# Storing the rows of a partial tile together, and dividing the last stores between two DMA queues

## The chip, the cores and the metric

The kernel runs on one core of a Trainium2 chip. The metric is the device time of one execution in microseconds (us). The engines that matter are TensorE (PE, matrix products), VectorE (DVE), ScalarE (ACT) and SyncE (SP). SP does no arithmetic: its queue issues DMA transfers. ScalarE's queue can issue them too, between its own instructions.

## The reference

A one-dimensional convolution with three taps over a sequence, batch normalisation with given statistics, and SiLU. B = 2, S = 2048, C = 1024, all bfloat16:

```python
xp = jnp.pad(x, ((0, 0), (1, 1), (0, 0)))
y = sum(jnp.einsum('bsc,cd->bsd', xp[:, k:k + S, :], w[k]) for k in range(3))
inv_std = 1.0 / jnp.sqrt(var + 1e-5)
y = (y - mean) * (g * inv_std) + b
return _silu(y)
```

## The kernel before

The convolution is computed by a minimal-filtering scheme: each group of R = 6 consecutive output rows needs eight products of transformed inputs and transformed weights instead of eighteen. A batch has NB = 342 such groups. As 2048 = 341 x 6 + 2, the last group holds only two rows; it is the partial tile of the change.

The inputs are loaded and transformed first. Then come 16 units of work, one for each block of 128 output channels (`dc`, eight) and batch (`bi`, two). `Unit.run` makes the eight products on TensorE, combines them on VectorE, and SiLU on ScalarE writes `yT`: 128 channels by 6 rows by 342 groups (padded to 384). The result has to be transposed before it is stored. The first 14 units do that with a DMA transpose (`turn`, line 439) and store with five DMAs (`store`, lines 451 and 455). The last two units are stored by `put` (line 409) instead: TensorE transposes 128 by 128 pieces into PSUM (line 419), VectorE or ScalarE copies them into a tile `o` (line 420), and each block of 128 groups is stored by one DMA (line 425).

The groups of a batch make three blocks: 0 and 1 of 128 groups and block 2 of 85 full groups and the partial one. `put` is called for `inner` rows 1 to 4 of each group and for `outer` rows 0 and 5, as these become ready at different times. Whenever a call covers the last block, it also stores the row of the partial group that its rows hold: row 1 in an inner call, row 0 in an outer call, one DMA of a single row of 256 bytes each (line 431).

The order of all instructions is written by hand; each engine runs its own in that order. The very last unit is cut in two halves, `h0` (groups 128 to 341, blocks 1 and 2) and `h1` (groups 0 to 127, block 0). The unit before it is `prev`. The kernel's last lines (526 to 539) call `put` for these three, and the last argument names the queue of each block's store, `sp` or `ac`.

Each DMA is given one of eight DMA semaphores by the framework. It is issued only once the previous DMA on the same semaphore has landed. In the built program the stores from line 533 on, with the number of the semaphore that each holds, are:

| queue | stores in order (semaphore) |
|---|---|
| SP | h0 inner block 1 (4), h0 inner block 2 (5), h0 row 1 (6), h0 outer block 1 (7), h0 outer block 2 (0), h0 row 0 (1), h1 outer (2) |
| ScalarE | h1 inner (2) |

A store of an inner block is 128 groups (85 in block 2) by 4 rows by 256 bytes, an outer one 2 rows. The four stores before these on SP are those of `prev`: outer block 2, row 0, inner block 2, row 1.

Of the kernel before, what the change touches and what calls it, by code (L numbers as in the profile page):

```python
# [15 lines left out]
P = 128  # L16
R = 6
# [9 lines left out]
def kernel(  # L27
# [11 lines left out]
    B, S, C = x.shape  # L39
# [29 lines left out]
    rows = consts.tile([4 * DC, P], BF16, name="rows")  # L69
# [217 lines left out]
    class Unit:  # L287
# [121 lines left out]
        def put(self, o, rows, bank, evac, queues, blocks=None):  # L409

            i0, i1 = min(rows), max(rows)
            every = slice(i0, i1 + 1, 1 if i1 == i0 else (i1 - i0) // (len(rows) - 1))
            blocks = blocks or range(self.lo // P, -(-self.hi // P))
            n = min(self.hi - self.lo, P)
            v = ps[:, bank].bitcast(BF16)[0:n, 0:len(rows) * len(blocks) * P]
            v = v.rearrange("p (i k d) -> p i k d", i=len(rows), k=len(blocks))
            for a, i in enumerate(rows):
                for q, k in enumerate(blocks):
                    nc.tensor.transpose(v[:, a, q], self.yT[:, i, k * P:k * P + n], ident)  # L419
            evac(o[0:n, every, blocks[0]:blocks[-1] + 1], v)  # L420
            outs = out[self.bi, :, self.dc * P:(self.dc + 1) * P]
            full = S // R
            for q, k in zip(queues, blocks):
                hi = min((k + 1) * P, full)
                q.dma_start(
                    out=outs[k * P * R:hi * R].rearrange("(p i) d -> p i d", i=R)[:, every],
                    in_=o[0:hi - k * P, every, k],
                )
                cut = [i for i in rows if i < S % R]
                if hi == full and cut:  # L430
                    q.dma_start(
                        out=outs[full * R + cut[0]:full * R + cut[-1] + 1].rearrange("(p i) d -> p i d", p=1),
                        in_=o[full - k * P:full - k * P + 1, cut[0]:cut[-1] + 1, k],
                    )

        def turn(self, pool=opool):

# [60 lines left out]
    for i, (dc, bi) in enumerate(seq[:-1]):  # L498
# [20 lines left out]
        before, prev = prev, unit  # L519
    dc, bi = seq[-1]  # L520
    sp, ac = nc.sync, nc.scalar
    inner, outer = tuple(range(1, R - 1)), (0, R - 1)
    to_v, to_s = nc.vector.tensor_copy, nc.scalar.copy
    o = olast.tile([P, R, NK, P], BF16, name="o")
    h0 = Unit(dc, bi, 4, P, NB)
    h0.run(between, prev.rest(between, 5, 5) + [(5, lambda: prev.put(o, inner, 1, to_v, (sp, sp), (0, 1)))])
    h1 = Unit(dc, bi, 0, 0, P)
    h1.run(between, [
        (2, lambda: prev.put(o, outer, 2, to_s, (sp, sp, sp))),
        (3, lambda: prev.put(o, inner, 1, to_s, (sp,), (2,))),  # L530
    ] + h0.rest(between, 5, 6))
    o2 = olast.tile([P, R, NK, P], BF16, name="o")
    h0.put(o2, inner, 5, to_v, (sp, sp))
    h1.silu_inner()
    h1.first(between)
    h1.last(between)
    h0.put(o2, outer, 6, to_v, (sp, sp))
    h1.put(o2, inner, 1, to_v, (ac,))
    h1.put(o2, outer, 2, to_v, (sp,))

_INS = ['x', 'w', 'mean', 'var', 'g', 'b']
_OUTS = [((2, 2048, 1024), 'bfloat16')]
# [24 lines left out]
```

## Time and profile before

| | |
|---|---|
| median of 3 runs | 193.5 us (193.17 to 193.84) |
| profiled execution | 193.33 us, span 191.6 us |
| mean granted TensorE clock | 0.991 |
| TensorE busy | 177.4 us, 93% of the span |
| VectorE, ScalarE busy | 156.8 us, 111.5 us |
| DMA moved | 31.71 MB |
| TensorE's last transpose ends | about 185.05 us |
| VectorE's last copy starts | 185.09 us |

The span runs from the first to the last instruction. Times in the timeline count from its start. A line of the timeline gives start, length, engine, line in the kernel and what is written from what; SPq and ACTq are the queues of SP and ScalarE, where the length of a DMA is that of its issue and not of its transfer. A line of the windows gives the stretch, its length, the busy time of PE, weight loads, DVE, ACT and POOL, the granted clock, the mean busy share of the 16 DMA engines and what they moved in GB/s. A line of the waits gives who waited for whom, the sum in us, the number of waits and the longest.

### The profile page before, as it was taken

To read this page: it belongs to the slowest core of one execution; us is meant where nothing else is said; L and a number is where in the kernel's file an instruction comes from. 1 tells how busy PE (TensorE), PEld (TensorE's weight loads), DVE (VectorE), ACT (ScalarE), POOL (GpSimd) and SP (SyncE) were. 2 spreads that over 40 slices of the span, in tenths; PEclk is the share of its full clock that TensorE was granted. 3 is DMA by queue.
4 is the path that set the end of the run, shared out by engine and by line. 5 is a ranking of instruction groups with operands and counts; after the bars stand their busy time and mean duration, and the time that the engine had idled before them with its cause. 6 is when DMAs were issued, how large, how long until landed. Compare 5 with 4: busy or idle time off the path is not lost.

```text
span 191.6 us, 3716 instructions
## 1 busy us (share of the span) xinstructions
PE 177.4 (93%) x1397; PEld 126.7 (66%) x1397; DVE 156.8 (82%) x222; ACT 111.5 (58%) x187; POOL 136.8 (71%) x76
## 2 busy tenths in 40 slices
PE   1998879999999999999999999999999999999960
PEld 1976758666666666666666666666666666678940
DVE  5589866789978799988998899879988996767960
ACT  3689977774546565465545554656274663636750
POOL 5579999806796879999999999699999780000000
PEclk9999999999999999999999999999999999999996
DMA  5999998084142838499759577969587396948652
GB/s 201 309 332 331 346 330 261 8 224 109 32 91 50 184 66 171 136 225 205 137 119 185 110 151 208 214 145 193 110 168 152 81 123 140 206 110 127 142 134 58
DMA packets 86800, 31.71 MB, mean 166 GB/s; under 512 B 73406, under 2 KB 82622, under 8 KB 86782
## 3 DMA queue, kind: packets, MB, share of 16 engines
q1 hardware_dynamic: 86190, 31.33, 71.8%
q8 instruction: 11, 0.18, 0.4%
q10 hardware_dynamic: 592, 0.14, 0.3%
q14 instruction: 7, 0.06, 0.1%
HBM read 14.82 MB, written 8.39 MB: 121 GB/s over the span
## 4 chain that ended last, share of the span: by engine, by line
PE 83%; DMA 7%; ACT 2%; SPq 2%; DVE 1%; issue 1%; ACTq 0%
PE ps L311 78%; DMA xw<-in_x_dram 6%; PE ps L265 5%; DMA rows<-in_g_dram 1%; SPq L130 1%; ACT T_sb L276 1%; PE ps L419 1%; DVE o L420 1%; ACT w1x L162 0%; DVE T_sb L278 0%; SPq L146 0%; ACTq L71 0%; ACT w1x L180 0%
## 5 line engine op out<-in xcount | busy, mean ns | idle before, releaser
L311 PE MATMUL ps<-T_sb,u 128*128 128x342 bf16 (+2 forms) x816 | 120.0, 299 | 0.3
L311 PEld LDWEIGHTS <-u 128*128 128x128 bf16 x816 | 76.8, 97 | 33.6 <-issue 0.6
L194 POOL TENSOR_TENSOR u<-e,w1x 128x1024 bf16<-128x1024 f32 x32 | 70.3, 2223 | 12.5 <-DVE e L176 12.4
L311 PE MATMUL ps<-T_sb,wch 128*128 128x342 bf16 (+2 forms) x272 | 42.5, 299 | 0.0
L334 ACT ACTIVATE yT<-ps,beta,scale 128x342 bf16<-128x342 f32 (+5 forms) x51 | 34.0, 704 | 11.8 <-PE ps L311 11.8
L329 DVE SCALAR_TENSOR_TENSOR t<-ps,sd 128x684 f32<-128x684 f32 (+2 forms) x51 | 39.1, 822 | 0.6
L194 POOL TENSOR_TENSOR u<-e,wch 128x1024 bf16<-128x1024 f32 x16 | 37.6, 2369 | 1.0 <-DMA wch<-in_w_dram 0.4
L311 PEld LDWEIGHTS <-wch 128*128 128x128 bf16 x272 | 25.7, 97 | 11.5
L322 ACT COPY pc<-ps 128x342 f32<-128x342 f32 (+2 forms) x34 | 14.5, 426 | 31.9 <-PE ps L311 31.2
L265 PE MATMUL ps<-rm,xw 128*128 128x168 bf16 (+1 forms) x256 | 26.1, 250 | 6.6 <-DVE rm L100 3.9
L276 ACT CAST T_sb<-ps 128x672 bf16<-128x672 f32 (+1 forms) x37 | 25.8, 735 | 7.4 <-PE ps L265 7.3
L278 DVE CAST T_sb<-ps 128x672 bf16<-128x672 f32 x29 | 23.5, 854 | 7.6 <-PE ps L265 7.6
L265 PEld LDWEIGHTS <-xw 128*128 128x128 bf16 (+1 forms) x256 | 21.4, 105 | 11.3 <-DMA xw<-in_x_dram 5.5
L329 DVE SCALAR_TENSOR_TENSOR ps<-ps,t 128x684 f32<-128x684 f32 (+2 forms) x34 | 28.3, 832 | 0.6
L176 DVE SCALAR_TENSOR_TENSOR e<-wch 128x1024 f32<-128x1024 bf16 x14 | 27.2, 1941 | 0.0
L329 DVE SCALAR_TENSOR_TENSOR ps<-ps,pc 128x342 f32<-128x342 f32 (+2 forms) x34 | 16.9, 498 | 8.9 <-PE ps L311 7.1
L174 POOL TENSOR_TENSOR e<-wch 128x1024 f32<-128x1024 bf16 x8 | 19.0, 2370 | 3.5 <-DMA wch<-in_w_dram 3.4
L334 ACT ACTIVATE yT<-t,beta,scale 128x684 bf16<-128x684 f32 (+2 forms) x17 | 15.7, 925 | 0.0
L329 DVE SCALAR_TENSOR_TENSOR sd<-pc,ps 128x342 f32<-128x342 f32 (+2 forms) x17 | 8.3, 487 | 8.4 <-ACT sd L322 8.3
L329 DVE SCALAR_TENSOR_TENSOR t<-ps,t 128x684 f32<-128x684 f32 (+2 forms) x17 | 13.9, 818 | 0.0
L322 ACT COPY sd<-ps 128x342 f32<-128x342 f32 (+2 forms) x17 | 7.3, 428 | 10.2 <-PE ps L311 10.2
L324 ACT ACTIVATE pc<-ps 128x342 f32<-128x342 f32 (+2 forms) x17 | 7.5, 440 | 9.4 <-PE ps L311 5.9
(39 smaller groups left out, 38.0 us busy)
## 6 DMA issues: line engine op xcount, KB each, us to landing
xw<-in_x_dram SPq DMA_DIRECT2D x30, 256.0 KB
out_dram<-o SPq DMA_DIRECT2D x28, 192.0 KB
wch<-in_w_dram SPq DMA_DIRECT2D x9, 512.0 KB
out_dram<-o SPq DMA_DIRECT2D x14, 120.0 KB
wch<-in_w_dram SPq DMA_DIRECT2D x6, 256.0 KB
xfirst<-in_x_dram SPq DMA_DIRECT2D x2, 224.0 KB
out_dram<-o SPq DMA_DIRECT2D x3, 128.0 KB
out_dram<-o SPq DMA_DIRECT2D x4, 64.0 KB
```

The lines of the kernel that those rows point to most:

```text
L130: nc.sync.dma_start(out=xw[0:hi - lo, :], in_=x[bi, lo:hi, :])
L174: eng.tensor_tensor(e, w0, w2, op=ALU.add)
L176: eng.scalar_tensor_tensor(out=e, in0=f, scalar=4.0, in1=h, op0=ALU.mult, op1=ALU.add)
L194: nc.gpsimd.tensor_tensor(u[:, i], sums[dc, q], o, op=op)
L265: nc.tensor.matmul(v[:, c * nb // nct, c % (nct // nb)], lhsT=xw[0:rows, (c0 + c) * P:(c0 + c + 1) * P], rhs=rm[0:rows, :, 0:n], start=Tru ...
L276: nc.scalar.copy(dst, src)
L278: nc.vector.tensor_copy(dst, src)
L311: nc.tensor.matmul(self.bank[q], lhsT=lhsT, rhs=T_sb[:, ct, j, nsl], start=not add and ct == 0, stop=ct == CT - 1, skip_group_check=add,)
L322: nc.scalar.copy(dst, self.bank[q])
L324: nc.scalar.mul(dst, self.bank[q], by)
L329: nc.vector.scalar_tensor_tensor(out=out, in0=in0, scalar=scalar, in1=in1, op0=ALU.mult, op1=op1)
L334: nc.scalar.activation(self.yT[:, rows, self.lo:self.hi], src, ACT.Silu, bias=beta[:, dc:dc + 1], scale=scale[:, dc:dc + 1])
```

## The change

`put` no longer stores rows of the partial group. A new method `put_cut` stores both of its rows by one DMA of two rows, once for `prev` and once for `h0`. Of the last unit's stores, h0's outer block 2 and h1's outer store are issued by ScalarE instead of SP.

```diff
@@ put
-                cut = [i for i in rows if i < S % R]
-                if hi == full and cut:
-                    q.dma_start(
-                        out=outs[full * R + cut[0]:full * R + cut[-1] + 1].rearrange("(p i) d -> p i d", p=1),
-                        in_=o[full - k * P:full - k * P + 1, cut[0]:cut[-1] + 1, k],
-                    )
+
+        def put_cut(self, o, queue):
+
+            full = S // R
+            k, p0 = full // P, full % P
+            queue.dma_start(
+                out=out[self.bi, full * R:S, self.dc * P:(self.dc + 1) * P].rearrange("(p i) d -> p i d", p=1),
+                in_=o[p0:p0 + 1, 0:S % R, k],
+            )
@@ the last unit
-        (3, lambda: prev.put(o, inner, 1, to_s, (sp,), (2,))),
+        (3, lambda: prev.put(o, inner, 1, to_s, (sp,), (2,))), (3, lambda: prev.put_cut(o, sp)),
...
     h0.put(o2, inner, 5, to_v, (sp, sp))
...
-    h0.put(o2, outer, 6, to_v, (sp, sp))
+    h0.put(o2, outer, 6, to_v, (sp, ac))
     h1.put(o2, inner, 1, to_v, (ac,))
-    h1.put(o2, outer, 2, to_v, (sp,))
+    h0.put_cut(o2, sp)
+    h1.put(o2, outer, 2, to_v, (ac,))
```

In the built program the stores of the last unit then stand as follows:

| queue | stores in order (semaphore) |
|---|---|
| SP | h0 inner block 1 (4), h0 inner block 2 (6), h0 outer block 1 (7), h0 two rows (0) |
| ScalarE | h0 outer block 2 (1), h1 inner (3), h1 outer (5) |

The stores of `prev` before these on SP are outer block 2, inner block 2 (semaphore 0) and its two rows (2). TensorE's, VectorE's and GpSimd's orders are as before.

## The prediction

> **What bounds the kernel now.** I read the page first, to see whether the change can touch the body. TensorE is busy for 177.4 us of the 191.6 us span, so the body is a TensorE chain. The changed lines only issue stores at the very end.
>
> ```profile
> span 191.6 us, 3716 instructions
> PE 177.4 (93%) x1397; PEld 126.7 (66%) x1397; DVE 156.8 (82%) x222; ACT 111.5 (58%) x187; POOL 136.8 (71%) x76
> ```
>
> So the tail is what counts. The chain of waits, in order of time, ends with VectorE's last copy into `o2`, at 185.09 + 0.29 = 185.4 us. The profile follows nothing past it, yet the span runs 6.2 us longer. In that time only stores are under way. The timeline of the tail, SP's queue and ScalarE's (start us, length us, queue, line):
>
> ```profile
> 183.18 0.25 SPq L431 DMA_DIRECT2D out_dram<-o  x1
> 183.54 0.28 SPq L425 DMA_DIRECT2D out_dram<-o  x1
> 183.87 0.42 SPq L431 DMA_DIRECT2D out_dram<-o  x1
> 184.39 0.39 SPq L425 DMA_DIRECT2D out_dram<-o  x1
> 184.84 0.39 SPq L425 DMA_DIRECT2D out_dram<-o  x1
> 185.09 0.42 ACTq L425 DMA_DIRECT2D out_dram<-o  x1
> 185.28 0.48 SPq L431 DMA_DIRECT2D out_dram<-o  x1
> 185.85 1.13 SPq L425 DMA_DIRECT2D out_dram<-o  x1
> 187.03 0.36 SPq L425 DMA_DIRECT2D out_dram<-o  x1
> 187.44 0.37 SPq L431 DMA_DIRECT2D out_dram<-o  x1
> 188.82 0.39 SPq L425 DMA_DIRECT2D out_dram<-o  x1
> ```
>
> The last line is the store of h1's outer rows. Its data have been ready since 185.4, but it is issued at 188.82, 3.4 us later. Two things hold it: SP's seven issues before it, which end at 187.81 (one of them takes 1.13), and then a wait. The waits of SP's queue from 187.5 on:
>
> ```profile
> SPq L425 <- DMA out_dram<-o: 0.9, 1, 0.9
> SPq L562 <- DMA out_dram<-o: 1.3, 1, 1.3
> ```
>
> The first is this store waiting for its DMA semaphore (number 2 of eight). ScalarE's store of 185.09, h1's inner rows, holds the same semaphore, and by the trace's record of semaphore increments its last one comes at 188.75. The second is the kernel's end waiting for the last store: from 189.26 to 190.49. Then 191.55 - 190.49 = 1.06 us of closing steps follow. The windows show the transfers (last two columns: share of the 16 DMA engines, GB/s):
>
> ```profile
> 184.50:185.00 0.50, 0.38 (x3) 0.17 (x2) 0.50 (x2) 0.27 (x1) 0.00 (x0) 1.00 0.33 71
> 185.50:186.00 0.50, 0.00 (x0) 0.00 (x0) 0.00 (x0) 0.00 (x0) 0.00 (x0) 1.00 0.87 198
> 188.50:189.00 0.50, 0.00 (x0) 0.00 (x0) 0.00 (x0) 0.00 (x0) 0.00 (x0) 0.50 0.12 26
> 189.00:189.50 0.50, 0.00 (x0) 0.00 (x0) 0.00 (x0) 0.00 (x0) 0.00 (x0) 0.50 0.02 5
> 189.50:190.00 0.50, 0.00 (x0) 0.00 (x0) 0.00 (x0) 0.00 (x0) 0.00 (x0) 0.50 0.48 112
> ```
>
> Traffic dies out by 189.5 and starts again for the late store alone. While only an 85-row store is moving (184.5 to 185.0), a third of the engines work, at 71 GB/s. A 128-row store uses all of them, at 198/0.87 = 228 GB/s. So 85-row stores load a narrow group of engines, and that group finishes last.
>
> **The change part by part.**
>
> *Four one-row stores go, two two-row stores come.* SP loses 0.25 + 0.42 + 0.48 + 0.37 = 1.52 us of issues. The nearest row for a two-row store is line 455, which has the same form: 14 issues of 640 to 647 ns. Two cost 1.28 us, so this part frees SP of 0.24 us. It is not on the path that sets the end.
>
> *h0's outer store of block 2 goes to ScalarE.* ScalarE's queue gets it before the store that it has now. VectorE's three last copies start at 184.25, 184.63 and 185.09, so its data are ready at 184.6. It can be issued at 184.65, for 0.36 us by its SP row. Its semaphore was last used by the 30-row store of 178.68, long landed. Behind it on ScalarE stand only two more stores, as all activations come earlier in that queue. The h1 inner store therefore still starts at about 185.09, when its copy ends.
>
> *h1's outer store goes to ScalarE.* It now follows the h1 inner store, at 185.09 + 0.42 + 0.05 = 185.56. The built program gives it semaphore 5, last used by a store of the unit before (issued 181.32, landed by 183.24). The 0.9 us wait is gone, and so is its place behind SP's issues. It is issued 3.26 us earlier, which would be the gain if nothing else were late. But the same bytes have to move.
>
> *What is late next: the narrow group.* Its time for each store, in full bytes (256 B a row piece): 85 x 4 pieces, 87 kB at 71 GB/s, 1.22 us; 85 x 2, 0.61; 128 x 4, 131 kB at 228 GB/s, 0.58; 128 x 2, 0.29.
> Test on the trace of before: the 85-row store issued at 183.54 starts to move at about 184.35 (18 GB/s in 184.0 to 184.5, then 71), 0.81 after its issue. Behind it the group has 1.22 + 0.58 + 1.22 + 0.58 + 0.29 + 0.61 = 4.50 us of work: it should end at 188.85. The row of 188.5 to 189.0 shows just that fall, to 26 GB/s.
> After the change, that store of the unit before takes the place of the one-row store at 183.18 (its copy has been done since 180.54), and moves from 183.18 + 0.81 = 184.0. The group has 0.29 more, the h1 outer store's share: 4.79 us, to 188.8. It doesn't starve: SP issues the two-row store at about 183.5 to 184.15, h0's inner stores at 184.2 and 184.65, h0's outer block 1 at 185.1, and ScalarE's are out by 186. Even an issue that is held up for 1.13 us meets a group with work waiting.
>
> *The trailing engine.* In before the stores of 187.03 and 187.44 land last at 189.47 and 189.65 by the increments, although the group's other engines have posted theirs by 189.01. One engine runs some 0.45 to 0.65 us behind. Its cause isn't settled: one-row stores that need this engine, or instruction loading (packets of 16 KB and 8 KB at 183.0 and 183.75 on the instruction queues, 0.88 and 0.42 us long). If the lag were all the one-row stores', the end would come at 189.0; if it stays, at 189.5 to 189.6. I take that it stays, as the 8 KB packet's 0.42 us is nearest to it: 189.65 - 0.05 (group end 188.8 instead of 188.85) = 189.6, less up to 0.2 as no one-row store stands last: 189.5.
>
> *h0's two-row store* waits for semaphore 0, which the unit before's 85-row store holds. That was issued at 183.54 in before and landed at 185.88, 2.34 us later; from 183.18 that gives 185.5, when SP's issue before it has just ended (185.5). It costs nothing then, and nothing but the kernel's end is behind it.
>
> *Sum.* The last landing moves from 190.47 to 189.5, by 1.0 us. The profiled execution took 193.33 (span 191.6 plus 1.7 around it): 192.3. The three runs have a median of 193.5, 0.17 above; I predict 192.4, between the two ends 192.3 and 192.5. Bounds of the gain: 1.5 (landing at 189.0), and 0.5 (the trailing engine another half us later, as much again as its lag now).
>
> **A rule weighed.** The row is the 3.4 us that finished data waited in SP's queue. The Trainium skill, page "DMA: Bandwidth & Descriptors", section "Issuing engines are not separate DMA queues", speaks against the change: stores started by several engines run on the same 16 DMA engines, and a second issuer saves only issuing time. By it the gain would be the issues moved off SP, 0.36 + 0.39 = 0.75 us, so 192.6. This trace agrees on shared engines, but not that only issuing is saved, for 0.9 us of the delay is a semaphore wait.
>
> **The rivals.**
>
> *More: the lag was the one-row stores'.* For it: they land up to 3.65 us after issue (185.28, at 188.93). Against: the instruction packets are as long as the lag. The end is at 189.0 or a little before, a gain of 1.5 to 1.8: 191.7 to 192.0. Chance 0.2.
>
> *Less: ScalarE's issues are held up.* For it: one SP issue took 1.13 us in this tail, and a store on line 451 1.44. Three in a row of 1.13 from 184.65 end at 188.1 with their gaps; the last store took 1.26 us from the end of its issue to landing (189.21 to 190.47) with idle engines; here it adds to the trailing engine, at up to 190.0. Gain 0.4 to 0.6: 192.9 to 193.1. Against: ScalarE's only store in this tail took 0.42. Chance 0.17.
>
> *Slower: the last two-row store ends the kernel.* It stands last on SP. If its issue, behind the full group, is held by 1.44 us twice (h0's outer block 1 and then itself, 185.1 to 188.0), and it then needs the 3.65 us that the one-row store of 185.28 needed from start to landing, 3.2 from the end of its issue, it lands at 191.2, 0.7 later than now: 194.0. It decides from a landing after 190.47. Against: that store's long time was the queue ahead of it, which by 188 is nearly empty. Chance 0.06.
>
> The change not doing what it says can be left out: the built order has both moves, and TensorE's and VectorE's orders are unchanged.
>
> **How the numbers follow.** The forecast, a gain of 0.6 to 1.5, has the remaining 0.57, its own range 192.0 to 192.9. Within 0.3% (0.58 us) is about what a measurement of this kernel can't tell from no change; the runs before alone spread by 0.35%. Faster: 0.57 + 0.2 and a third of the second rival, less a little for that spread: 0.81. Slower: 0.05. Same: 0.14. The range for 8 in 10 runs from 191.6 (the first rival, less 0.1 of run to run) to 193.1 (most of the second).
>
> **What would show it.** ScalarE's queue with three line-425 stores at about 184.65, 185.1 and 185.6; no SP wait of 0.9 on line 425; full-width traffic ending by 188, a thin tail to 189.2, and no second burst; the closing wait ending at about 189.5. It is wrong if ScalarE's issues stretch past 187, if the closing wait ends after 190, or if a fall in the span comes from before 183.

## The result and the profile after

The changed kernel takes 192.66 us (median of 13 runs, 192.02 to 193.34) against 193.5 us before (13 runs). The ratio is 0.9952, with a 95% interval of 0.9932 to 0.9973: 0.9 us faster, between 0.5 and 1.3. The profiled execution took 192.30 us with a span of 190.5 us.

TensorE and the other engines do the same work as before:

```profile
span 190.5 us, 3715 instructions
PE 177.3 (93%) x1397; PEld 126.5 (66%) x1397; DVE 157.6 (83%) x222; ACT 111.2 (58%) x187; POOL 136.8 (72%) x76
```

In this execution VectorE's last copy into `o2` ends at 185.17, 0.21 earlier than in the one of before. That is drift between executions: the code ahead of it is the same, and over all executions below this copy ends between 185.2 and 186.5. So two tails are compared from the end of that copy. From there to the last landing it is 190.47 - 185.38 = 5.09 us before and 189.56 - 185.17 = 4.39 us after. (Landings, here and below, are read from the trace's record of semaphore increments; a store adds up to 16 of them, one for each DMA engine that it runs on; a store on fewer engines has one entry more, ahead of these, which isn't counted here.)

The timeline of the tail, first SP's queue from the store of `prev`'s inner block 2 on, then ScalarE's (start us, length us, queue, line):

```profile
183.28 0.27 SPq L425 DMA_DIRECT2D out_dram<-o  x1
183.61 0.64 SPq L434 DMA_DIRECT2D out_dram<-o  x1
184.35 0.40 SPq L425 DMA_DIRECT2D out_dram<-o  x1
185.23 0.28 SPq L425 DMA_DIRECT2D out_dram<-o  x1
185.60 0.53 SPq L425 DMA_DIRECT2D out_dram<-o  x1
186.18 1.30 SPq L434 DMA_DIRECT2D out_dram<-o  x1
184.49 0.30 ACTq L425 DMA_DIRECT2D out_dram<-o  x1
184.89 0.52 ACTq L425 DMA_DIRECT2D out_dram<-o  x1
185.50 0.48 ACTq L425 DMA_DIRECT2D out_dram<-o  x1
```

The last issue starts at 186.18 where it started at 188.82. It is the two-row store of h0, and it is held for 1.30 us. h1's outer store, the last line, goes out at 185.50. The waits of SP's queue from 182.5 on:

```profile
SPq L566 <- DMA out_dram<-o: 2.0, 2, 1.5
SPq L425 <- DMA out_dram<-o: 0.5, 1, 0.5
```

The first is the closing wait: SP has issued everything by 187.5 and waits for landings until 189.59. The second is new. h0's inner block 2 waits for semaphore 6, whose holder was issued at 181.89; 15 of its increments are there by 183.64, the last comes at 185.21.

The windows (last two columns: busy share of the 16 DMA engines, GB/s):

```profile
186.50:187.00 0.50, 0.00 (x0) 0.00 (x0) 0.00 (x0) 0.00 (x0) 0.00 (x0) 1.00 0.99 225
187.50:188.00 0.50, 0.00 (x0) 0.00 (x0) 0.00 (x0) 0.00 (x0) 0.00 (x0) 0.50 0.52 112
188.00:188.50 0.50, 0.00 (x0) 0.00 (x0) 0.00 (x0) 0.00 (x0) 0.00 (x0) 0.50 0.37 83
188.50:189.00 0.50, 0.00 (x0) 0.00 (x0) 0.00 (x0) 0.00 (x0) 0.00 (x0) 0.50 0.32 71
189.00:189.50 0.50, 0.00 (x0) 0.00 (x0) 0.00 (x0) 0.00 (x0) 0.00 (x0) 0.50 0.02 3
189.50:190.00 0.50, 0.00 (x0) 0.00 (x0) 0.00 (x0) 0.00 (x0) 0.00 (x0) 0.50 0.00 0
```

The second burst of before, 112 GB/s in 189.5 to 190.0, is gone. In its place the last microsecond runs on a third of the engines, at 71 to 83 GB/s: the narrow group, working off its queue. The stores land at 188.94 (h0 inner block 2), 189.15 (h1 outer), 189.39 (h0 outer block 1) and 189.56 (the two rows).

So the time is won in the tail. Which of the two edits won it, and what limits the tail now, is what the experiments ask.

### The profile page after: what moved, and what is told of

It reads as the page before. It is cut to its first block, busy times and chain, and to the rows that moved or that the text cites. A ratio compares the mean times of both kernels' runs of the same rounds, so it can differ in the third digit from the quotient of the medians.

```text
span 190.5 us, 3715 instructions
## 1 busy us (share of the span) xinstructions
PE 177.3 (93%) x1397; PEld 126.5 (66%) x1397; DVE 157.6 (83%) x222; ACT 111.2 (58%) x187; POOL 136.8 (72%) x76
## 4 chain that ended last, share of the span: by engine, by line
PE 82%; DMA 5%; ACT 4%; DVE 3%; SPq 2%; issue 1%; DVEq 0%
PE ps L311 76%; PE ps L265 5%; DMA xw<-in_x_dram 5%; DVE T_sb L278 3%; ACT yT L334 2%; SPq L130 2%; ACT T_sb L276 1%; SPq L146 1%; PE ps L419 1%; ACT w1x L162 0%; ACT o L420 0%; DVE o L420 0%; ACT w1x L180 0%; ACT pc L322 0%; DVEq L278 0%
## 5 line engine op out<-in xcount | busy, mean ns | idle before, releaser
L176 DVE SCALAR_TENSOR_TENSOR e<-wch 128x1024 f32<-128x1024 bf16 x14 | 28.0, 2000 | 0.0
```

Of the source, the lines that this page charges most:

```text
L176: eng.scalar_tensor_tensor(out=e, in0=f, scalar=4.0, in1=h, op0=ALU.mult, op1=ALU.add)
```

## The experiments

Two theories on the gain. A: the late store was late because of a semaphore that it shared with h1's inner store, and a change that breaks the sharing wins the gain; what is left is the narrow group's work. B: the gain comes from dividing the stores between two queues, as SP's was too long.

### Only the merged store

From the changed kernel, the two queue edits are undone:

```diff
-    h0.put(o2, outer, 6, to_v, (sp, ac))
+    h0.put(o2, outer, 6, to_v, (sp, sp))
...
-    h1.put(o2, outer, 2, to_v, (ac,))
+    h1.put(o2, outer, 2, to_v, (sp,))
```

> Only the one-row stores are merged; all queues are as before, so h1's outer store stands last on SP. Theory A (the end is set by when the last store may be issued and by the narrow group's bytes, and the semaphore wait is what mattered): merging alone changes which semaphore the last store holds (0, whose holder before it lands by about 185.9), so the 0.9 us wait is gone without any change of queue. SP issues it after the two-row store, at 187.5 to 188.1 instead of 188.82, landing at 189.2 to 189.8: 0.6 to 1.2 us faster than before, ratio 0.994 to 0.997. Theory B (the division between the queues makes the gain): only SP's issue time is saved, 0.24 us, ratio 0.999.

Measured: ratio to before 0.9947 (0.9918 to 0.9976). All of the changed kernel's gain is here, with no store moved between queues. SP's last three issues:

```profile
186.37 0.92 SPq L425 DMA_DIRECT2D out_dram<-o  x1
187.34 0.60 SPq L434 DMA_DIRECT2D out_dram<-o  x1
188.04 0.39 SPq L425 DMA_DIRECT2D out_dram<-o  x1
```

The wait ahead of the last one is gone. h1's outer store follows the two-row store at once, 188.04 - 185.69 = 2.35 us after the last copy, against 3.44 before. Its semaphore had been free since 186.33. The issues ahead of it end 2.25 us after the last copy, against 2.43 before, so of the 1.09 us some 0.2 are issuing and the rest is the wait. Merging two rows of 256 bytes acts on the time mainly through the numbering of the semaphores. The landing gains less in this execution: 15 of the last store's increments are there by 189.69, within the 189.2 to 189.8 that A gave, but the sixteenth comes at 190.32, 4.6 us after the last copy.

This run also tells something of the trailing engine. There are no one-row stores in this tail, and one engine of the narrow group still trails: of h0's inner block 2 four increments are there by 188.54 and the last comes at 189.30.

### Every store on SP

From the kernel before, the other way round: ScalarE issues nothing in the tail.

```diff
-    h1.put(o2, inner, 1, to_v, (ac,))
+    h1.put(o2, inner, 1, to_v, (sp,))
```

> Before, with every store of the last unit on SP: nothing is issued by ScalarE at all, the one-row stores stay. The eight semaphores then go round on one queue, and h1's outer store no longer shares one with h1's inner store. Theory A (the semaphore wait made the loss, not the length of SP's queue): SP issues h1's inner store after the one-row store, at about 187.9, and h1's outer at 188.3 instead of 188.82; it lands at 189.9 to 190.2, 0.3 to 0.6 us faster than before although SP has more to do, ratio 0.997 to 0.9985. Theory B (the division between the queues makes the gain): one more store on SP, 0.4 us slower than before or worse, ratio 1.002 and up.

Measured: ratio 0.9941 (0.9911 to 0.997). It is faster than expected, and B's 1.002 is outside the interval. SP's last three issues:

```profile
187.22 0.38 SPq L431 DMA_DIRECT2D out_dram<-o  x1
187.69 0.39 SPq L425 DMA_DIRECT2D out_dram<-o  x1
188.19 0.45 SPq L425 DMA_DIRECT2D out_dram<-o  x1
```

SP issues one store more than before, and h1's outer store still goes out 188.19 - 185.58 = 2.6 us after the last copy instead of 3.4, as the eight semaphores now go round in the order of one queue and none is waited for. Not all of this is the semaphore: h0's outer block 1 took 0.39 us to issue here and 1.13 before. From the last copy to the last landing it is 4.39 us, as in the changed kernel. In the kernel before it was the one store on ScalarE that made the two share a semaphore.

### Only the queues, and only the last store

Both start from the kernel before and keep the one-row stores. The first divides the queues as the change does:

```diff
-    h0.put(o2, outer, 6, to_v, (sp, sp))
+    h0.put(o2, outer, 6, to_v, (sp, ac))
...
-    h1.put(o2, outer, 2, to_v, (sp,))
+    h1.put(o2, outer, 2, to_v, (ac,))
```

> Only the queues are divided; the one-row stores stay (row 0 of h0 goes to ScalarE with its block). Theory A: h1's outer store is out by 186.2, but the semaphores fall differently: h0's outer block 1 on SP now waits for semaphore 2, which ScalarE's h0 outer block 2 holds until it lands at about 187. It is issued at about 187.1 and lands at about 189.0, when the narrow group ends anyway: closing wait ends at 189.3 to 189.7, 0.8 to 1.2 us faster than before, ratio 0.994 to 0.996. Theory B says the same size, 0.994 to 0.996; a theory that the one-row stores are the delay (they trail by 0.45 to 0.65) says 0.998 to 1.000.

Measured: 0.9973 (0.9947 to 1.0), less than either theory gave, though the interval reaches into what all three gave, so this run doesn't part them. The waits of SP's queue from 183 on show a new wait:

```profile
SPq L562 <- DMA out_dram<-o: 2.1, 1, 2.1
SPq L425 <- DMA out_dram<-o: 1.6, 1, 1.6
```

It isn't the one that I had expected. h0's inner block 1 has fallen on semaphore 6, held by `prev`'s outer block 1. That store has 15 increments by 184.24 and the sixteenth at 186.45. So SP stands still from 184.89 to 186.52, with h0's stores behind. One late engine of an earlier store holds SP's queue for 1.6 us here, because the semaphore numbers fell so.

The second moves h1's outer store alone:

```diff
-    h1.put(o2, outer, 2, to_v, (sp,))
+    h1.put(o2, outer, 2, to_v, (ac,))
```

> Before, with h1's outer store alone moved to ScalarE. Theory A: the wait is handed on. h0's row 0, last on SP, now gets semaphore 2 and has to wait for ScalarE's h1 inner store until about 188.75, so a store of 256 bytes ends the kernel, landing at 190.0 to 190.5: 0 to 0.5 us faster than before, ratio 0.9975 to 1.000. Theory B (SP's queue was too long; taking one store off it helps): 0.8 to 1.0 us faster, ratio 0.995.

Measured: 0.9985 (0.9964 to 1.0005). The size is the one that A gave, and B's 0.995 lies outside the interval. But A's way to it isn't in the trace. h0's row 0 goes out at 188.67, directly behind the issue before it; its semaphore was free from 188.43. What SP waited for was once more semaphore 6, 0.6 us before h0's inner block 2. In the profiled execution the last landing comes 4.37 us after the last copy, as good as in the changed kernel, which the 12 runs' ratio doesn't repeat. This run shows that the move alone doesn't bring the change's gain; it doesn't show why.

### What limits the tail now: leaving out one store

From the changed kernel, one of h0's two inner stores is left out: block 2 (85 by 4 pieces of 256 bytes) or block 1 (128 by 4).

```diff
-    h0.put(o2, inner, 5, to_v, (sp, sp))
+    h0.put(o2, inner, 5, to_v, (sp,))
```

> The changed kernel without h0's inner store of block 2 (85 by 4 pieces, 87 kB); these rows of the output are left out. Theory A (the narrow group's bytes set the end): 1.22 us of the group's work goes, so the last landing moves 0.8 to 1.2 us earlier, as far as the two-row store's issue lets it: ratio to before 0.989 to 0.992, 0.003 to 0.006 below the changed kernel. If the end is set by issuing alone, one issue of 0.28 us goes: ratio 0.994.

```diff
-    h0.put(o2, inner, 5, to_v, (sp, sp))
+    h0.put(o2, inner, 5, to_v, (None, sp))
...
             for q, k in zip(queues, blocks):
+                if q is None:
+                    continue
```

> The changed kernel without h0's inner store of block 1 (128 by 4 pieces, 131 kB); these rows of the output are left out. Theory A: half as much as without the 85-row store, though half as many bytes again are left out: 0.58 us of the group's work, the last landing 0.3 to 0.6 earlier, ratio to before 0.992 to 0.994. If bytes in all set the end, it gains more than the other leave-out: 0.989 or below.

Measured: 0.9872 (0.9831 to 0.9912) without the 85-row store, 0.9913 (0.9885 to 0.994) without the 128-row store. Against the changed kernel's 0.9952 these are 1.5 us and 0.75 us. The store with two thirds of the bytes is worth twice as much, which is the proportion of the narrow group's times, 1.22 to 0.58. Both are some 0.2 to 0.3 us more than the group's work alone. The two intervals overlap, and both runs have a new wait before h0's outer block 1, for semaphore 6 (0.9 and 1.2 us), so the times alone don't settle it; the traces say more. Without the 85-row store the windows end wide:

```profile
187.50:188.00 0.50, 0.00 (x0) 0.00 (x0) 0.00 (x0) 0.00 (x0) 0.00 (x0) 1.00 1.05 236
188.00:188.50 0.50, 0.00 (x0) 0.00 (x0) 0.00 (x0) 0.00 (x0) 0.00 (x0) 1.00 0.94 228
188.50:189.00 0.50, 0.00 (x0) 0.00 (x0) 0.00 (x0) 0.00 (x0) 0.00 (x0) 0.77 0.61 147
189.00:189.50 0.50, 0.00 (x0) 0.00 (x0) 0.00 (x0) 0.00 (x0) 0.00 (x0) 0.50 0.00 0
```

Nearly all engines are busy to the end and there is no thin stretch. In this execution the last copy ended at 186.51, so the end is 2.86 us after it instead of 4.39. Without the 128-row store a thin stretch stays, 0.28 of the engines at 62 GB/s in 188.0 to 188.5, and the end is 3.68 us after the last copy. By the tails too the smaller store takes more off, 1.53 us against 0.71, which a limit by bytes in all wouldn't give.

### Taking the load off the narrow group

If the group is the limit, the 85-row stores should be cut to 80 rows, as 80 is a multiple of 16 and can go to all engines (in the run they show 16 increments), and as `store` already cuts them. The five groups left over, of all six rows, get one store ahead of the two-row store.

```diff
-                hi = min((k + 1) * P, full)
+                hi = min((k + 1) * P, full // 16 * 16)
...
         def put_cut(self, o, queue, other=None):
...
+            lo = full // 16 * 16
+            (other or queue).dma_start(
+                out=out[self.bi, lo * R:full * R, self.dc * P:(self.dc + 1) * P].rearrange("(p i) d -> p i d", i=R),
+                in_=o[p0 - (full - lo):p0, :, k],
+            )
```

> The changed kernel, with the 85-row stores cut to 80 rows, and the last five full groups stored by one DMA of 5 by 6 rows ahead of the two-row store. Theory A (the narrow group's bytes set the end of the changed kernel): of the 85-row stores only a small part stays on the group; its work falls from 4.8 us to about 2.9, below what the issues allow. The two-row store is issued last at 186.7 to 187.3 and lands at 188.0 to 188.7: 0.8 to 1.5 us faster than the changed kernel, 1.8 to 2.4 faster than before, ratio 0.988 to 0.991. If the end is set by issues or by the two-row store itself, it is no better than the changed kernel: 0.995, or worse for the added DMA: 0.996 to 0.998.

Measured: 0.9992 (0.9972 to 1.0013), worse than the changed kernel. Theory A's expectation failed by far, and the timeline of SP's queue says how:

```profile
184.01 1.15 SPq L425 DMA_DIRECT2D out_dram<-o  x1
185.21 0.85 SPq L435 DMA_DIRECT2D out_dram<-o  x1
186.11 0.63 SPq L439 DMA_DIRECT2D out_dram<-o  x1
186.84 0.41 SPq L425 DMA_DIRECT2D out_dram<-o  x1
...
189.28 0.64 SPq L439 DMA_DIRECT2D out_dram<-o  x1
```

The last unit's first store (the fourth line) goes out at 186.84, 1.00 us after the last copy. In the changed kernel it went out 0.82 us before that copy ended. `prev`'s three stores ahead of it take 1.15 + 0.85 + 0.63 us to issue. The 0.85 is the added store; the 1.15 is the 80-row store, whose 85-row form took 0.27 in the changed kernel, and why it is held isn't known. The transfers themselves are wide now:

```profile
187.00:187.50 0.50, 0.00 (x0) 0.00 (x0) 0.00 (x0) 0.00 (x0) 0.00 (x0) 1.00 0.76 173
188.00:188.50 0.50, 0.00 (x0) 0.00 (x0) 0.00 (x0) 0.00 (x0) 0.00 (x0) 1.00 0.88 212
188.50:189.00 0.50, 0.00 (x0) 0.00 (x0) 0.00 (x0) 0.00 (x0) 0.00 (x0) 1.00 0.85 182
```

They start late instead. The limit has gone from the narrow group to SP's issues, and these cost some 0.8 us more than the group did. Here SP's queue was too long, which it wasn't in the kernel before.

So the same kernel, with both small stores of both units on GpSimd, which has nothing to do in the tail:

```diff
-    ... (3, lambda: prev.put_cut(o, sp)),
+    ... (3, lambda: prev.put_cut(o, nc.gpsimd)),
...
-    h0.put_cut(o2, sp)
+    h0.put_cut(o2, nc.gpsimd)
```

> The 80-row stores again, with the store of 5 by 6 rows and the two-row store, for both units, issued by GpSimd, which is idle in the tail. In the 80-row kernel SP was late by its own issues (0.85 and 0.64 us for the two small stores, h0's inner block 1 out at 186.84 instead of 184.35). Theory A: with these issues off SP and little work on the narrow group, h0's and h1's stores are out by 186.7 and landed by 188.0 to 188.8: ratio to before 0.987 to 0.991. If GpSimd's small stores take longer than SP's, they end the kernel: 0.994 to 1.000; if narrow and wide stores make no difference, 0.995 as in the changed kernel.

Measured: 0.9909 (0.9878 to 0.994), 1.8 us faster than before and 0.8 faster than the changed kernel by the ratios. The last landing is 3.40 us after the last copy. SP's stores:

```profile
183.78 0.32 SPq L425 DMA_DIRECT2D out_dram<-o  x1
184.20 0.41 SPq L425 DMA_DIRECT2D out_dram<-o  x1
184.66 1.25 SPq L425 DMA_DIRECT2D out_dram<-o  x1
186.56 0.39 SPq L425 DMA_DIRECT2D out_dram<-o  x1
```

and the windows of its end:

```profile
187.00:187.50 0.50, 0.00 (x0) 0.00 (x0) 0.00 (x0) 0.00 (x0) 0.00 (x0) 1.00 1.04 207
187.50:188.00 0.50, 0.00 (x0) 0.00 (x0) 0.00 (x0) 0.00 (x0) 0.00 (x0) 1.00 1.03 234
188.00:188.50 0.50, 0.00 (x0) 0.00 (x0) 0.00 (x0) 0.00 (x0) 0.00 (x0) 0.54 0.26 55
```

Wide until 188, and nothing moves after 188.5. What is late next is the last line of SP's queue: h0's outer block 1, which waited 0.6 us for semaphore 6 and its one late engine (186.50), and lands last at 188.94. This is the fastest version of this study that stores every row.

To part the two edits, the changed kernel with only its two-row stores on GpSimd:

```diff
-    h0.put_cut(o2, sp)
+    h0.put_cut(o2, nc.gpsimd)
```

(and the same for `prev`).

> The changed kernel with its two two-row stores issued by GpSimd; the 85-row stores stay as they are. It parts the gain of the 80-row kernel on GpSimd (0.9909) between the two edits. Theory A (the narrow group's bytes set the end): the group has the same 4.8 us of work from the same start, so little is gained: the two-row store no longer lands last, 0.1 to 0.3 us, ratio to before 0.9935 to 0.995. If SP's issues were the limit, all of the gain comes from this edit: 0.991 or below.

Measured: 0.9947 (0.9922 to 0.9973), no better than the changed kernel within the interval. Each of the two edits alone gains nothing over the changed kernel (0.9992 and 0.9947); together they gain 0.8 us. The reading that fits is that each takes away one of two limits. It is argued, not shown: in this run h0's outer block 1 also waited 1.0 us for semaphore 6, more than any store did in the changed kernel.

## Why the prediction was right

The forecast was 192.4 us with a range of 191.6 to 193.1; the time is 192.66. The gain came at 0.9 us by the ratio where the sum gave 1.0. Step by step:

- *The tail is what counts.* Right. The engines' busy times are the same, and the gain lies after the last copy: 5.09 - 4.39 = 0.7 us there in the two profiled executions, 0.2 more of their difference in span is drift ahead of it, and 0.1 the closing steps.
- *The 0.9 us wait for semaphore 2.* Right, and the core of it. The wait is gone in the changed kernel, and in the two experiments that break the sharing in other ways and bring no new wait (0.9947 and 0.9941).
- *Its place behind SP's issues.* I counted this beside the wait as something that the move to ScalarE saves. It is worth nothing here: with everything on SP the kernel is as fast. The move of the two stores, which reads as the larger half of the change, gains nothing that the merging doesn't gain alone. I had the right cause, a semaphore, but tied it to the wrong edit.
- *The narrow group is late next.* Right: the two leave-outs support it, by their windows more than by their times. Its end was put at 188.8; traffic falls at 189.0. The group started 0.1 later than I had put it.
- *h0's inner stores at 184.2 and 184.65.* The second went out at 185.23, held 0.5 us by semaphore 6. I had looked up the landing of the two-row store's semaphore and of h1's, not of this one. By the windows it cost nothing, as the group had other work; no run takes this wait away alone.
- *The trailing engine.* Wrong in its term, right in its sum, and that is luck. I kept its 0.45 to 0.65 us in the end, and the end came at 189.56 where I put 189.5. But no engine of the group trails in the last stores after the change. This time the late engine is outside the group: it shows in the store of 181.89, a 128-row store, with its last increment 1.6 us late. What fills its place is a group end 0.2 later and the two-row store, 0.17 behind all others.
- *h0's two-row store costs nothing.* Nearly: its issue was held 1.30 us, and it is the last to land. Two two-row stores cost SP 1.95 us, not 1.28, more than the 1.52 that the one-row stores took. In the run with only the merged stores they cost 0.64 + 0.60 = 1.24, so 1.28 was a fair price and the held issue is what it left out.
- *Two readings were off, and nothing rests on them.* The instruction packets start at 183.16 and 183.96, not at 183.0 and 183.75, and of the last unit's stores six stand ahead of h1's outer store on SP, not seven.

The rivals. "More", that the lag was the one-row stores', fell: with these merged and the queues as before, an engine of the group still trails by 0.8 us. "Less", ScalarE's issues held up, did not come: they took 0.30, 0.52 and 0.48. "Slower", the two-row store ends the kernel, came in its place but not at its price: held once for 1.30, it landed 2.1 us after the end of its issue and not 3.2, since the queue ahead of it was nearly done.

The rule weighed from the Trainium skill, "DMA: Bandwidth & Descriptors", section "Issuing engines are not separate DMA queues", gave 192.6 by the issuing time moved off SP. The time agrees with that sum, but not its reason: with no store moved to ScalarE the gain is the same, so here not even issuing time was worth anything. As a rule on bandwidth it stands: before, SP's stores alone moved 198 GB/s at a share of 0.87 of the engines; after, in 186.5 to 187.0, where by the packets nearly all is ScalarE's, it is 225 at 0.99. That is 228 and 227 at a full share: the same engines.

## What to carry to other kernels

When the last store of a kernel goes out long after its data were ready, look at what its queue waits for before moving it to another queue: here it was a DMA semaphore shared with a store of another queue, and the two edits that ended the sharing and brought no new wait won some 0.5%, even the one that put more on the slow queue. Then look at the waits that the new numbering brings: the change itself brought one of 0.5 us and won as much, but the two edits that brought waits of 0.6 and 1.6 us won only 0.15% and 0.3%, neither clear of nothing. Why waits of 0.5 and 0.6 us before the same store went with such different gains stays open. Count a tail of stores twice, by the issues of each queue and by the work of the fewest DMA engines that its stores use, since an edit that mends one of two limits may show nothing. A store of 85 partitions ran on a third of the engines, at 71 GB/s; cutting it at a multiple of 16 paid only when the small remainder had a queue with time for it.

## What the runs showed of the hardware

- One DMA engine runs late in this tail in every trace, by up to 2.2 us on stores that use all 16 (15 increments by 184.24 and the sixteenth at 186.45, with only the queues divided). Of the ten kernels after the first, seven waited for such a store: semaphore 6, held by `prev`'s outer block 1, was waited for by 0.5 to 1.6 us. In time it goes with two packets on the instruction queues, of 16 KB (0.88 to 1.4 us) and 8 KB (0.3 to 0.6 us). That these cause it is argued from their times; it wasn't tried, as the instruction stream can't be shortened without changing the work. Whether the late engine belonged to the narrow group differed between the executions.
- The length of an issue isn't a matter of its size. A two-row store of 512 bytes took 0.64 us where a store of 128 by 4 pieces took 0.40. Some issues are held: 1.13, 1.15, 1.25 and 1.30 us were seen, on one store each in four of these tails. How busy the engines are doesn't tell which: during these issues they were busy for 0.70, 0.21, 0.81 and 0.92 of the time. The cause is open.
- A store lands with the latest of its engines, so a narrow store can land before a wide one that was issued ahead of it on the same queue: in the changed kernel the 128-row store of 181.89 had 15 increments by 183.64 and landed at 185.21, and the 85-row store of 182.42 landed at 184.35.
